# Moving the start addresses of the tiles that TensorE reads

## The chip, the cores and the metric

One core of one Trainium2 chip runs the whole program in one launch. The metric is the device time of one execution in microseconds (us). The kernel before has a median of 933.54 us over 2 runs (933.08 to 934.0).

## What is computed

Three layers follow each other: a gated linear attention (4 batches, 8 heads, 768 steps, head width 48), and two two-layer networks over 3072 tokens. Cut to what matters:

```python
for t in range(S):                       # attention
    state = f[:, :, t, :, None] * state + k_t (outer) v_t
    y[:, :, t] = q_t @ state
x = y as [3072 tokens, 384]
g = softplus(x @ w_in1);   x = g @ w_out1        # 384 -> 2048 -> 384
h = x @ w_in2                                     # 384 -> 2048
g = where(h >= 1, h, where(h <= -1, 0, (h + 1)**2 / 4))
out = g @ w_out2                                  # 2048 -> 384
```

## The kernel before

**Tiling.** Tokens go in six blocks of 512 per network. The 2048 hidden columns are 16 chunks of 128. For one chunk of one block, `hmm` (line 726) forms the hidden tile of 128 x 512 from the input (three pieces of 128 rows), `act1` or `act2` applies the nonlinearity on ScalarE and VectorE, and `second` (lines 800 to 802) multiplies the result into three output tiles that accumulate over the 16 chunks.

**Split numbers.** Every operand is kept as a high part and a low remainder, each in the type float32r: the input in `xh` and `xl` (one tile `xhl`), the hidden tile in `gh` and `gl` (three buffers each), the weights of chunk c in `w_h[c]` and `w_l[c]`. A product is three matmuls: low weights by high data, high weights by high data, high weights by low data. So a chunk of a block costs 9 matmuls in `hmm` and 9 in `second`, each with 128 x 128 weights and 512 moving columns. A weight tile holds 768 columns: 384 for the first product and 384 for the second. Block 0 of the first network is the exception: its operands are plain float32 (`xr2`, `g_0`, lines 726 and 805), with one matmul instruction pair in the place of three matmuls.

**Which weights are read where.** The first network uses `w_h[c]`, `w_l[c]` for all 16 chunks. The second network uses six further pairs, `wxh` and `wxl`, for chunks 0 to 5, and `w_h[c - 6]`, `w_l[c - 6]` for chunks 6 to 15. The `wx` tiles are allocated in `release()` in the space that the attention tiles leave.

**Order.** `Order` collects all operations with planned costs, due times and dependences between named tiles, schedules them once, and emits them in that order. The planned costs and the names do not depend on addresses. DMAs are all issued on SP's queue.

**Addresses.** Tiles of a pool lie one behind the other in each partition. Up to the small tiles at the end of the pool `const`, every tile is a multiple of 512 bytes long. In the placed program `xhl` starts at byte 2208, which is 160 modulo 512; so `w_h`, `w_l`, `stg`, `gh`, `gl`, `te`, `tu`, `tl`, `xr2`, `wa` and `g_0` all start at 160 modulo 512 as well. The attention tiles and later `acc`, `wxh` and `wxl` start at 352 modulo 512 (one attention tile, `ks1`, at 96).

The functions that the change touches:

Of the kernel before, what the change touches and what calls it, by code (L numbers as in the profile page):

```python
# [8 lines left out]
F32 = mybir.dt.float32  # L9
F32R = mybir.dt.float32r  # L10
# [7 lines left out]
P = 128  # L18
# [6 lines left out]
TB = 512  # L25

LAG, GB, TE = 2, 3, 2
# [289 lines left out]
def attn_moe_moe2_kernel(ctx: ExitStack, tc: tile.TileContext, q, k, v, f_logit,  # L317
# [8 lines left out]
    NFC = FF // P  # L326
# [4 lines left out]
    WN = NK * P + DM  # L331
# [5 lines left out]
    const = mstack.enter_context(tc.tile_pool(name="const", bufs=1))  # L337
# [7 lines left out]
    def buf(name, shape, n, dt=F32, pool=const):  # L345
        return [pool.tile(shape, dt, name=f"{name}{i}", tag=f"{name}{i}") for i in range(n)]
# [20 lines left out]
    H2 = [3, 5, 1]  # L367
    O2 = [4, 7, 6]

    xhl = const.tile([P, 2, NK, XR], F32R, name="xhl")  # L370
    xh, xl = xhl[:, 0], xhl[:, 1]
    yT = dram.tile([DM, NT], F32, name="yT")
    w_h = buf("wh", [P, WN], NFC, F32R)
    w_l = buf("wl", [P, WN], NFC, F32R)
    stg = buf("stg", [P, WN, 2] if wide else [P, WN], 2, I32 if wide else F32)
    g_h = buf("gh", [P, TB], GB, F32R)
    g_l = buf("gl", [P, TB], GB, F32R)
    t_e = buf("te", [P, TB], TE)
    t_u = buf("tu", [P, TB], 1)
    t_l = buf("tl", [P, TB], TE)  # L380
# [73 lines left out]
    w2x, acc = [], []  # L454
# [460 lines left out]
    def release():  # L915
        astack.close()
        wx = mstack.enter_context(tc.tile_pool(name="w2x", bufs=1))
        acc.append(wx.tile([P, TB], F32, name="acc"))
        nc.gpsimd.memset(acc[0], 0.0)
        for c in range(NX):  # L920
            w2x.append((wx.tile([P, WN], F32R, name=f"wxh{c}"), wx.tile([P, WN], F32R, name=f"wxl{c}")))

    conv2 = 0
    wnext = 2
# [1 line left out]
    for i in range(len(steps) + LAG):  # L926
        if i < len(steps):
            L, bi, t0, N, c = steps[i]
# [37 lines left out]
        if not released and ndone[0] == NU:  # L966
            released = True
            held = sorted((x for x in attn_keys if x[0] not in ("bank", "xh", "xl", "xr2", "x0", "te", "tl", "tu", "gh")), key=str)
            do("none", 0, release, held, [("w2x",), ("acc",)] + held)
            s_of[2, 0], s_of[2, 1] = load_w(2, 0), load_w(2, 1)  # L970
        j = i - LAG
        if j >= 0:
            L, bi, t0, N, c = steps[j]
# [66 lines left out]
```

## Time and profile before

| | |
|---|---|
| median of 2 runs | 933.54 us (933.08 to 934.0) |
| the profiled execution's own time | 934.49 us |
| its span, first to last instruction | 932.8 us |
| TensorE matmul (PE) busy | 915.6 us, 98% of the span |
| TensorE weight loads (PEld) busy | 711.9 us, 76% |
| VectorE (DVE) busy | 656.5 us, 70% |
| ScalarE (ACT) busy | 638.0 us, 68% |
| GpSimd (POOL) busy | 71.9 us, 8% |
| granted TensorE clock | 0.998 of full speed |

PE and PEld are one engine: a weight load runs beside the matmul before it. A matmul is pipelined: its record starts when it is taken up and ends when its last result is out, so the records of neighbours overlap, and a mean duration is longer than the time from one start to the next. The ends of matmuls in the records are modelled. What a stream of matmuls costs is read from the starts.

### The profile page before, as it was taken

What the parts mean: (1) busy time and instruction counts of PE and PEld (TensorE: products, weight loads), DVE (VectorE), ACT (ScalarE), POOL (GpSimd) and SP (SyncE); (2) the same over time, 40 slices, a digit from 0 to 9 for tenths busy, and PEclk for the clock granted to TensorE, in tenths of its full rate; (3) what the DMA queues carried; (4) which work ended last, traced back from release to release, by engine and by line L of the source; (5) the groups of instructions that cost most, each with busy time, mean ns of one, the idle gap of its engine ahead of it and who ended that gap; (6) DMA issues with size and microseconds to landing.
All of it is one profiled execution on the core that took longest, in us unless ns stands there. A gap on an engine that the chain in (4) does not pass through costs nothing.

```text
span 932.8 us, 14237 instructions
## 1 busy us (share of the span) xinstructions
PE 915.6 (98%) x5480; PEld 711.9 (76%) x5480; DVE 656.5 (70%) x1030; ACT 638.0 (68%) x1145; POOL 71.9 (8%) x91
## 2 busy tenths in 40 slices
PE   8999999999999999999999999999999999999997
PEld 7634458778778787788877888888888888888885
DVE  7999999877877777658999974464454554544542
ACT  5567689678777786667787778888864544544443
POOL 0001011001001000100020010020010010100000
PEclk9999999999999999999999999999999999999999
DMA  9577761412221221201343366665610200200001
GB/s 280 187 250 248 233 213 57 134 49 91 62 64 58 85 63 35 69 1 34 103 136 102 102 204 200 207 209 196 222 50 1 68 0 1 69 1 1 34 1 38
DMA packets 86540, 96.95 MB, mean 104 GB/s; under 512 B 4544, under 2 KB 66496, under 8 KB 86464
## 3 DMA queue, kind: packets, MB, share of 16 engines
q1 hardware_dynamic: 86464, 95.96, 31.7%
q8 instruction: 45, 0.74, 0.3%
q14 instruction: 31, 0.25, 0.1%
HBM read 80.22 MB, written 9.44 MB: 96 GB/s over the span
## 4 chain that ended last, share of the span: by engine, by line
PE 88%; DVE 6%; DMA 2%; issue 1%; ACT 1%; POOL 0%; SPq 0%; DVEq 0%; ACTq 0%
PE bank L726 40%; PE bank L800 12%; PE bank L801 12%; PE bank L802 12%; PE bank L805 3%; PE bank L625 3%; PE bank L667 1%; PE bank L681 1%; PE bank L654 1%; PE bank L672 1%; DVE gl L771 1%; DVE tl L763 1%; DMA xr<-yT 1%; DVE te L761 1%; PE bank L605 1%
## 5 line engine op out<-in xcount | busy, mean ns | idle before, releaser
L726 PE MATMUL bank<-xhl,wh 128*128 128x512 f32 x840 | 259.5, 390 | 0.0
L726 PEld LDWEIGHTS bank<-xhl,wh 128*128 128x128 f32 x840 | 157.7, 188 | 32.2 <-issue 0.2
L726 PE MATMUL bank<-xhl,wl 128*128 128x512 f32 x420 | 168.4, 401 | 0.4 <-DVE tl L763 0.4
L802 PE MATMUL bank<-gl,wh 128*128 128x512 f32 x420 | 163.7, 390 | 1.7 <-DVE gl L771 1.7
L800 PE MATMUL bank<-gh,wl 128*128 128x512 f32 x420 | 164.2, 391 | 0.0
L801 PE MATMUL bank<-gh,wh 128*128 128x512 f32 x420 | 163.5, 389 | 0.0
L424 ACT CAST gh<-tl 128x512 fp32r<-128x512 f32 x176 | 108.8, 618 | 73.2 <-DVE tl L786 51.1
L786 DVE TENSOR_TENSOR tl<-bank,te 128x512 f32<-128x512 f32 x96 | 66.3, 692 | 70.4 <-ACT te L785 70.4
L788 DVE TENSOR_TENSOR gl<-tl,gh 128x512 fp32r<-128x512 f32 x96 | 69.7, 727 | 61.8 <-ACT gh L424 60.2
L756 ACT ACTIVATE te<-bank 128x512 f32<-128x512 f32 x96 | 57.0, 594 | 60.9 <-PE bank L726 60.6
L726 PEld LDWEIGHTS bank<-xhl,wl 128*128 128x128 f32 x420 | 78.8, 188 | 22.0 <-DVE tl L763 2.9
L781 ACT ACTIVATE te<-bank 128x512 f32<-128x512 f32 x96 | 57.1, 594 | 54.0 <-PE bank L726 53.5
L802 PEld LDWEIGHTS bank<-gl,wh 128*128 128x128 f32 x420 | 78.8, 188 | 19.2 <-DVE gl L771 2.6
L800 PEld LDWEIGHTS bank<-gh,wl 128*128 128x128 f32 x420 | 78.8, 188 | 17.2 <-ACT gh L424 0.3
L801 PEld LDWEIGHTS bank<-gh,wh 128*128 128x128 f32 x420 | 78.9, 188 | 16.2
L785 ACT ACTIVATE te<-te 128x512 f32<-128x512 f32 x96 | 60.5, 631 | 41.5 <-DVE te L783 41.5
L761 DVE SCALAR_TENSOR_TENSOR te<-tu,te 128x512 f32<-128x512 f32 x96 | 68.1, 709 | 27.8 <-ACT tu L420 27.5
L783 DVE TENSOR_SCALAR te<-te 128x512 f32<-128x512 f32 x96 | 44.1, 460 | 55.3 <-ACT te L781 55.1
L771 DVE TENSOR_TENSOR gl<-tl,gh 128x512 fp32r<-128x512 f32 x80 | 56.6, 708 | 22.3 <-ACT gh L424 21.6
L763 DVE SCALAR_TENSOR_TENSOR tl<-bank,tl 128x512 f32<-128x512 f32 x96 | 65.7, 684 | 5.6 <-ACT tl L759 5.6
L726 PE MATMUL bank<-xhl,wxh 128*128 128x512 f32 x216 | 66.9, 391 | 0.0
L420 ACT ACTIVATE tu<-te 128x512 f32<-128x512 f32 x96 | 60.6, 631 | 2.3 <-DVE te L761 0.4
(115 smaller groups left out, 1378.6 us busy)
## 6 DMA issues: line engine op xcount, KB each, us to landing
stg<-in_moe_w_in_dram SPq DMA_DIRECT2D x64, 384.0 KB, 3.7
stg<-in_moe_w_out_dram SPq DMA_DIRECT2D x64, 384.0 KB, 4.4
t_f<-in_f_logit_dram SPq DMA_DIRECT2D x23, 256.0 KB, 3.5
t_k<-in_k_dram SPq DMA_DIRECT2D x23, 256.0 KB, 3.5
t_q<-in_q_dram SPq DMA_DIRECT2D x23, 256.0 KB, 3.7
vz<-in_v_dram SPq DMA_DIRECT2D x23, 256.0 KB, 3.9
wl<-wa SPq DMA_DIRECT2D x14, 384.0 KB, 3.0
yT<-xr SPq DMA_DIRECT2D x18, 256.0 KB, 3.3
```

Of the source, the lines that this page charges most:

```text
L420: "act": (c_act(n), lambda: nc.scalar.activation(out=o, in_=x, func=AF.Identity, bias=1.0))}
L424: "act": (c_act(n, ps), lambda: nc.scalar.copy(o(), x()))}
L726: nc.tensor.matmul(o, l, r, start=(j == 0), stop=(j == n - 1))
L761: do("dve", c_dve(N), lambda: nc.vector.scalar_tensor_tensor(out=e, in0=u, scalar=-1.0, in1=e, op0=ALU.add, op1=ALU.subtract), [ku, ke], [ke])
L763: do("dve", c_dve(N), lambda: nc.vector.scalar_tensor_tensor(out=l, in0=h, scalar=0.0, in1=l, op0=ALU.max, op1=ALU.add), [kb, kl], [kl])
L771: do("dve", c_dve(N), lambda: nc.vector.tensor_tensor(out=gl, in0=l, in1=gh.bitcast(F32), op=ALU.subtract), [kl, kgh], [kgl])
L785: do("act", c_act(N), lambda: nc.scalar.activation(out=r, in_=r, func=AF.Square), [kr], [kr])
L786: do("dve", c_dve(N), lambda: nc.vector.tensor_tensor(out=l, in0=h, in1=r, op=ALU.max), [kb, kr], [kl])
L788: do("dve", c_dve(N), lambda: nc.vector.tensor_tensor(out=gl, in0=l, in1=gh.bitcast(F32), op=ALU.subtract), [kl, kgh], [kgl])
L800: nc.tensor.matmul(o, ol, gh, start=(c == 0), stop=False)
L801: nc.tensor.matmul(o, oh, gh, start=False, stop=False)
L802: nc.tensor.matmul(o, oh, gl, start=False, stop=(c == NFC - 1))
```

## The change

The tiles get other start addresses; no instruction is added, removed or reordered by the source. An unused tile of 352 bytes is placed ahead of `xhl`, so that `xhl` starts at 0 modulo 512. Each weight tile becomes 32 bytes longer, each `gh` and `gl` tile 64 bytes longer, and the kernel uses slices of the old length. The `wx` tiles get the same 32 bytes.

```diff
+    const.tile([P, 88], F32, name="pad")
     xhl = const.tile([P, 2, NK, XR], F32R, name="xhl")
...
-    w_h = buf("wh", [P, WN], NFC, F32R)
-    w_l = buf("wl", [P, WN], NFC, F32R)
+    w_h = [x[:, 0:WN] for x in buf("wh", [P, WN + 8], NFC, F32R)]
+    w_l = [x[:, 0:WN] for x in buf("wl", [P, WN + 8], NFC, F32R)]
...
-    g_h = buf("gh", [P, TB], GB, F32R)
-    g_l = buf("gl", [P, TB], GB, F32R)
+    g_h = [x[:, 0:TB] for x in buf("gh", [P, TB + 16], GB, F32R)]
+    g_l = [x[:, 0:TB] for x in buf("gl", [P, TB + 16], GB, F32R)]
...
-            w2x.append((wx.tile([P, WN], F32R, name=f"wxh{c}"), wx.tile([P, WN], F32R, name=f"wxl{c}")))
+            w2x.append([wx.tile([P, WN + 8], F32R, name=f"wx{x}{c}")[:, 0:WN] for x in "hl"])
```

Adding up the lengths gives the starts after it, modulo 512: `xhl` 0; `w_h[c]` and `w_l[c]` 32c each; `stg` 0; `gh` 0, 64, 128; `gl` 192, 256, 320; `te`, `tu`, `tl`, `xr2`, `wa` and `g_0` 384; `wxh` of chunk c 64 + 64c and `wxl` 96 + 64c; the attention tiles 64 (`ks1` 320). In all 1,760 bytes more of each partition are used.

## Rows read from the trace of the kernel before

**Rows 1.** The page: busy us (share of the span) and instructions of two engines.
```profile
PE 915.6 (98%) x5480; PEld 711.9 (76%) x5480; DVE 656.5 (70%) x1030; ACT 638.0 (68%) x1145; POOL 71.9 (8%) x91
```

**Rows 2.** The page: chain that ended last, shares of the span by engine.
```profile
PE 88%; DVE 6%; DMA 2%; issue 1%; ACT 1%; POOL 0%; SPq 0%; DVEq 0%; ACTq 0%
```

**Rows 3.** Busy time by stretch: us, engines with instructions, granted clock, DMA share, GB/s.
```profile
0.00:112.00 112.00, 104.52 (x784) 60.44 (x784) 105.70 (x169) 69.30 (x116) 10.18 (x23) 1.00 0.75 239
112.00:485.00 373.00, 372.05 (x2774) 291.27 (x2773) 303.11 (x473) 289.18 (x517) 34.90 (x51) 1.00 0.26 82
485.00:545.00 60.00, 57.88 (x250) 46.16 (x250) 59.76 (x89) 44.37 (x77) 3.44 (x3) 1.00 0.35 113
545.00:932.80 387.80, 381.18 (x1677) 314.00 (x1675) 187.97 (x302) 235.21 (x437) 23.37 (x15) 1.00 0.25 85
```

**Rows 4.** Matmul groups by shape: count, busy us, mean ns of one, idle before.
```profile
L726 PE MATMUL bank<-xhl,wh 128*128 128x512 f32 x840 | 259.5, 390 | 0.0
L801 PE MATMUL bank<-gh,wh 128*128 128x512 f32 x420 | 163.5, 389 | 0.0
...
L726 PE MATMUL bank<-xhl,wxh 128*128 128x512 f32 x216 | 66.9, 391 | 0.0
L801 PE MATMUL bank<-gh,wxh 128*128 128x512 f32 x108 | 42.5, 394 | 0.0
...
L726 PE MATMUL bank<-xhl,wxl 128*128 128x512 f32 x108 | 42.3, 392 | 0.0
L802 PE MATMUL bank<-gl,wxh 128*128 128x512 f32 x108 | 41.9, 388 | 0.0
```

**Rows 5.** Timeline of PE, second network: start us, us; last matmul of a chunk.
```profile
569.31 0.39 PE L802 MATMUL bank<-gl,wh 128*128 128x512 f32 x1
...
593.79 0.39 PE L802 MATMUL bank<-gl,wh 128*128 128x512 f32 x1
...
606.11 0.39 PE L802 MATMUL bank<-gl,wxh 128*128 128x512 f32 x1
...
618.47 0.39 PE L802 MATMUL bank<-gl,wxh 128*128 128x512 f32 x1
```

**Rows 6.** Timeline of PE in the plain float32 block, six instructions merged.
```profile
103.69 2.74 PE L726 MATMUL bank<-xr,wl 128*128 128x512 f32 x6
```

**Rows 7.** The costliest groups of the page: the float32 matmuls of that block.
```profile
L726 PE MATMUL bank<-xr,wl 128*128 128x512 f32 x96 | 44.1, 595 | 0.6 <-ACT xr L424 0.6
```

**Rows 8.** Timelines of PE and PEld where the next weight load comes late.
```profile
162.34 0.39 PE L802 MATMUL bank<-gl,wh 128*128 128x512 f32 x1
162.65 0.30 PE L667 MATMUL bank<-am,vz 128*32 128x128 f32 x1
...
162.11 0.19 PEld L802 LDWEIGHTS bank<-gl,wh 128*128 128x128 f32 x1
162.65 0.38 PEld L667 LDWEIGHTS bank<-am,vz 128*32 128x32 f32 x16 [0.35 <-issue]
```

**Rows 9.** Timeline of PE after a stall, and its group in that window.
```profile
449.49 0.40 PE L726 MATMUL bank<-xhl,wh 128*128 128x512 f32 x1
449.73 0.39 PE L726 MATMUL bank<-xhl,wh 128*128 128x512 f32 x1
...
L726 PE MATMUL bank<-xhl,wh 128*128 128x512 f32 x1 | 0.4, 397 | 0.0
```

**Rows 10.** VectorE's split of a weight tile: count, busy us, mean ns, idle before.
```profile
L500 DVE TENSOR_TENSOR wl<-wa,wh 128x768 fp32r<-128x768 f32 x10 | 9.5, 953 | 0.1
L500 DVE TENSOR_TENSOR wxl<-wa,wxh 128x768 fp32r<-128x768 f32 x6 | 5.7, 949 | 0.6 <-ACT wxh L424 0.6
```

**Rows 11.** DMA issues: count, KB each, median us from issue to landing.
```profile
stg<-in_moe_w_in_dram SPq DMA_DIRECT2D x64, 384.0 KB, 3.7
wl<-wa SPq DMA_DIRECT2D x14, 384.0 KB, 3.0
```

## The prediction, made before the changed kernel was run

> **What bounds the kernel now.** I read the busy shares first: PE is busy for 98% of the span, the next engine, VectorE, for 70% [rows 1]. The chain that ended last says the same: 88% of it is PE [rows 2]. Then the stretches, since an average can hide a stage: PE is full in all four, and VectorE equals it only in two short ones, the first 112 us (105.70 of 112) and the 60 us between the networks (59.76 of 60) [rows 3]. So the time is the number of matmuls times the time from one matmul to the next, and an edit of addresses matters if it changes that interval. The granted clock is 1.00 in every stretch, the upper of the two levels (2.4 GHz) [rows 3], so the clock is no unknown.
>
> The matmuls that the change is about are the float32r ones. Eleven blocks (five of the first network, six of the second) of 16 chunks with 18 each are 3,168. Of these 648 read `wx` weights (6 blocks x 6 chunks x 18: one group of 216 and four of 108) and 2,520 read `w` weights (one group of 840 and four of 420) [rows 4].
>
> The interval comes from starts. Between the last matmuls of two `w` chunks, 569.31 and 593.79, lie six chunks or 108 matmuls: 24.48 / 108 = 226.7 ns. Between 606.11 and 618.47 lie three `wx` chunks or 54 matmuls: 12.36 / 54 = 228.9 ns [rows 5]. 3,168 matmuls at 227 ns are 719 us, 77% of the span.
>
> **A natural experiment in the trace.** In all of the kernel before, moving data and `w` weights start at the same address modulo 512, while `wx` weights start 192 bytes away from the moving data. That is the thing the change varies, and the price is there: 2.2 ns more per matmul, not less. The mean durations agree: 388 to 394 ns with `wx`, against 389 in the undisturbed `w` group [rows 4]. So a different start is not shown to be better; the only other start in the trace is slightly worse.
>
> Why the effect is small can be estimated from the shapes. One matmul reads 2,048 bytes per partition, so it passes every address modulo 512 four times; a weight load reads 512 bytes and passes each once. Whatever the two starts, the streams cross; the starts set only when.
>
> **The change part by part.**
>
> *Weights of the `w` chunks at 32c.* Chunk 0 of the first network and chunk 6 of the second (which reads tile 0) keep the offset of 0 to `xhl`: 5 x 18 + 6 x 18 = 198 matmuls, which I leave as they are (their `gh` and `gl` move too; the size of that is inside the bounds). The other 2,322 get an offset that is not 0. No row shows most of these offsets. From below: the `gl,wxh` group at 388 ns is the shortest, 1 ns under 389 [rows 4], so 2,520 x -1 = -2.5 us. From above: a matmul just after a stall, when load and matmul meet at another moment, took 397 ns and 0.24 us to the next start [rows 9]: 8 ns more, 2,520 x 8 = +20.2 us. The longest steady group, `gh,wxh` at 394 [rows 4], gives 2,520 x 5 = +12.6 us. I take 2.2 ns, the only steady value at an unequal offset: 2,322 x 2.2 = **+5.1 us**.
>
> *Weights of the `wx` chunks.* They go from one unequal offset to others. Bounds: all at the `w` interval, 648 x -2.2 = -1.4 us; all at 397 ns against their mean of 391, 648 x 6 = +3.9 us. I take **0**.
>
> *Moving data at 0 in place of 160.* No float32r matmul in the trace has moving data elsewhere, so its own price is unknown. Above nothing I have no row but the 397 already counted; below, the float32 block sets the bound: six instructions last 2.74 us [rows 6], less one duration of 0.595 [rows 7] that is 2.145 / 5 = 429 ns per instruction with two passes of 512 columns, 214.5 ns per pass. A float32r pass takes 12.2 ns more. But that block's moving tiles and weights stand at 160 too, and pay nothing for it. And a matmul that starts at 162.34 with no weight load beside it until 162.65 has the same 0.39 us as every other [rows 8]. So neither 160 as such nor the load beside it explains the 12 ns as far as rows go (with the reserve that ends are modelled). I take **0**, and keep the 12 ns for a rival.
>
> The Trainium skill, "TensorE: Matmul & The Clock Gate", section "Step-by-step: what each phase is for", says that TensorE reads moving data and weights through two independent ports, so that loading the next weights takes nothing from the running matmul. By that the sum would be 0. It speaks against the change. The trace agrees where a matmul without a load is no shorter [rows 8], and disagrees by the 2.2 ns of `wx` [rows 5].
>
> *The float32 block and the attention.* 192 instructions with moving data at 384 and weights at 32c. They have slack: two passes per load, and 214.5 ns per pass. At 5 ns per instruction it would be 1 us; I take 0. The attention tiles all move together by 224 bytes, so their offsets to each other stay.
>
> *VectorE, ScalarE, DMA.* VectorE's split takes 953 ns into tiles at 160 and 949 at 352 [rows 10]: nothing. PE hides them except between the networks, where VectorE fills 60 us [rows 3]; 1% there is 0.6 us. Weight transfers land in 3.7 and 3.0 us [rows 11], and DMA holds 2% of the chain [rows 2]: a tenth more or less on that, 932.8 x 0.02 x 0.1, is 2 us at most. The same DMAs go out on SP's queue in the same order, and no wait is added, since the planner's costs and tile names don't depend on addresses; the unused tile emits no instruction.
>
> **Sum.** +5.1 us. The profiled execution took 934.49 us, 1.7 more than its span and 0.95 more than the median of 933.54. Against the median: 933.54 + 5.1 = 938.6. The likeliest case's own range, from the lower bounds together (-2.5 - 1.4) to the steady upper bound (+12.6 and 1.7 for `wx`), is 929.6 to 947.8.
>
> **The rivals.**
>
> *No effect.* Within a nanosecond the interval doesn't depend on starts, and `wx` is slower for another reason, such as its place high in the partition. For: the crossing argument. Against: nothing else separates `wx` from `w` in the trace. Time: 933.5.
>
> *Faster.* The 12.2 ns between float32r and the float32 pass is a collision of equal or ill-placed starts, and goes: 2,520 x 12.2 + 648 x 14.4 = 40 us. Between the networks VectorE takes over [rows 3], where 250 matmuls would have brought 3 us. 933.5 - 37 = 897 at best, 915 if half of the offsets profit. For: the gap exists, and float32r is the only kind that shows it. Against: [rows 8], and `wx` with an unequal offset is no faster. The skill's page named above, section "Back-to-back issue gap", gives N / 2.4 + 2.5 ns, 215.8 for 512 columns; by it the interval of 226.7 leaves 11 ns to win, which the float32 pass agrees with and no float32r row here shows.
>
> *Slower.* Many of the 15 new offsets hold load and matmul in the bad meeting that now occurs only after stalls, at 397 ns [rows 9]. The place is every float32r matmul; the price 20.2 + 3.9 = 24 us, 957.6. It decides from a mean of 18.7 / 3,168 = 5.9 ns per matmul upward. For: the `wx` groups already range over 388, 392 and 394. Against: even they average under 3 ns.
>
> *It doesn't do what it says.* Other starts than added up would need a placement that rounds by more than 32 bytes; then the time is the no-effect one, and its chance is in that.
>
> **How the numbers follow.** About 2% (18.7 us) is what a measurement of this kernel can tell from no change. Forecast 0.50, no effect 0.22, faster rival 0.16 (of which 0.02 stays within 2%), slower rival 0.12. So faster 0.14, same 0.74, slower 0.12. The range of 928 to 953 takes in the likeliest case, no effect and the near part of the slower rival; it leaves out the faster rival and the far end of the slower one, 0.2 together.
>
> **What would show it.** The durations by tile: `wh` and `wl` groups near 391 instead of 389, `wx` near 391, and PE's interval in six `w` chunks near 24.7 us instead of 24.48. Chunks should differ from each other, since each has its own offset. The float32 instruction stays at 429 ns from start to start. I am wrong if the float32r interval falls below 225 ns (the 12 ns were a matter of address), or if the mean passes 233 (the bad meeting is the common one). If PE's interval is unchanged and the time is not, the cause lies in DMA or in the stretch between the networks.

## The result, and the profile after

The changed kernel takes 945.76 us (945.57 to 945.94, 2 runs) against 933.54 us: a ratio of 1.0131, 95% interval 1.0087 to 1.0174. It is slower by 12.2 us, a small loss but one clear of the noise. Its profiled execution has a span of 943.8 us, 11.0 us more than before. In its code, line 726 has become 728, and 800 to 802 have become 802 to 804.

The page of the changed kernel: busy us, share and instructions of the engines, and the chain's shares by engine (answers to [rows 1, 2]).

```profile
PE 928.4 (98%) x5480; PEld 713.1 (76%) x5480; DVE 656.9 (70%) x1030; ACT 639.4 (68%) x1145; POOL 76.2 (8%) x91
...
PE 93%; DVE 3%; DMA 1%; issue 1%; ACT 1%; POOL 0%; SPq 0%; DVEq 0%; POOLq 0%
```

The same number of instructions, 12.8 us more of PE, and VectorE, ScalarE and the weight loads within 1.4 us of what they were. PE's share of the chain grows from 88% to 93%. The time is in the matmuls.

The busy time by stretch of the changed kernel (columns as in [rows 3]) says the same: PE stays full and the granted clock stays 1.00. The stretches are cut by time, so they don't hold the same work as before.

```profile
0.00:112.00 112.00, 104.95 (x784) 60.96 (x785) 105.89 (x170) 69.30 (x116) 12.43 (x23) 1.00 0.74 241
112.00:485.00 373.00, 372.20 (x2754) 287.90 (x2753) 299.93 (x468) 286.10 (x511) 33.08 (x50) 1.00 0.26 81
485.00:545.00 60.00, 58.78 (x253) 46.98 (x252) 59.74 (x89) 45.05 (x78) 7.53 (x3) 1.00 0.31 99
545.00:943.80 398.80, 392.46 (x1693) 317.22 (x1691) 191.36 (x307) 238.92 (x442) 23.20 (x15) 1.00 0.25 85
```

The groups of float32r matmuls (answer to [rows 4]): count, busy us, mean ns of one, idle before.

```profile
L728 PE MATMUL bank<-xhl,wh 128*128 128x512 f32 x840 | 263.2, 394 | 0.0
L728 PE MATMUL bank<-xhl,wl 128*128 128x512 f32 x420 | 169.9, 405 | 0.0
L802 PE MATMUL bank<-gh,wl 128*128 128x512 f32 x420 | 165.8, 395 | 0.0
L804 PE MATMUL bank<-gl,wh 128*128 128x512 f32 x420 | 165.7, 394 | 1.2 <-DVE gl L773 1.2
L803 PE MATMUL bank<-gh,wh 128*128 128x512 f32 x420 | 165.6, 394 | 0.0
L728 PE MATMUL bank<-xhl,wxh 128*128 128x512 f32 x216 | 67.6, 394 | 0.0
...
L804 PE MATMUL bank<-gl,wxh 128*128 128x512 f32 x108 | 42.6, 394 | 0.0
L728 PE MATMUL bank<-xhl,wxl 128*128 128x512 f32 x108 | 42.5, 394 | 0.0
L803 PE MATMUL bank<-gh,wxh 128*128 128x512 f32 x108 | 42.5, 394 | 0.0
```

Before, the `w` groups stood at 389 to 391 ns and the `wx` groups between 388 and 394. Now all stand near 394. The one exception, `xhl,wl`, holds some 40 matmuls of about 500 ns that open a chunk, in both kernels, and has risen likewise, from 401 to 405. Before it was:

```profile
L726 PE MATMUL bank<-xhl,wl 128*128 128x512 f32 x420 | 168.4, 401 | 0.4 <-DVE tl L763 0.4
```

Some 4 ns on 2,520 matmuls and some 2.3 ns on 648 make 11.6 us, against 11.0 us more span. The starts in the two traces say the same: the 3,123 intervals from one float32r matmul to another right behind it add up to 719.7 us before and 731.2 after.

The timeline of PE gives the interval. These are the same four matmuls of the second network as in [rows 5].

```profile
573.53 0.39 PE L804 MATMUL bank<-gl,wh 128*128 128x512 f32 x1
...
598.63 0.39 PE L804 MATMUL bank<-gl,wh 128*128 128x512 f32 x1
...
611.16 0.40 PE L804 MATMUL bank<-gl,wxh 128*128 128x512 f32 x1
...
623.66 0.40 PE L804 MATMUL bank<-gl,wxh 128*128 128x512 f32 x1
```

Six `w` chunks: 25.10 us / 108 = 232.4 ns from start to start, where it was 226.7. Three `wx` chunks: 12.50 / 54 = 231.5 ns, where it was 228.9. So in both the interval has grown as the durations have: a steady 389 ns stands for 226.7 ns, and a duration longer by d for an interval longer by d. The experiments below are read by that.

"Offset" below means the start of the weights less the start of the moving data, so `wx` had 192 before. The direction counts: 192 and 64 are not the same offset.

The float32 block didn't move (answer to [rows 6], timeline of PE):

```profile
103.51 2.74 PE L728 MATMUL bank<-xr,wl 128*128 128x512 f32 x6
```

### The profile page after: what moved, and what is told of

Its sections match the earlier page's. It is cut to its first block, busy times and chain, and to the rows that moved or that the text cites. A ratio compares the mean times of both kernels' runs of the same rounds, so it can differ in the third digit from the quotient of the medians.

```text
span 943.8 us, 14237 instructions
## 1 busy us (share of the span) xinstructions
PE 928.4 (98%) x5480; PEld 713.1 (76%) x5480; DVE 656.9 (70%) x1030; ACT 639.4 (68%) x1145; POOL 76.2 (8%) x91
## 4 chain that ended last, share of the span: by engine, by line
PE 93%; DVE 3%; DMA 1%; issue 1%; ACT 1%; POOL 0%; SPq 0%; DVEq 0%; POOLq 0%
PE bank L728 42%; PE bank L802 13%; PE bank L804 13%; PE bank L803 13%; PE bank L807 3%; PE bank L627 3%; PE bank L669 1%; PE bank L683 1%; PE bank L656 1%; PE bank L674 1%; PE bank L607 1%; DMA stg<-in_moe_w_in_dram 1%; PE bank L678 0%; PE bank L530 0%; DMA t_f<-in_f_logit_dram 0%
## 5 line engine op out<-in xcount | busy, mean ns | idle before, releaser
L728 PE MATMUL bank<-xhl,wh 128*128 128x512 f32 x840 | 263.2, 394 | 0.0
L804 PE MATMUL bank<-gl,wh 128*128 128x512 f32 x420 | 165.7, 394 | 1.2 <-DVE gl L773 1.2
L803 PE MATMUL bank<-gh,wh 128*128 128x512 f32 x420 | 165.6, 394 | 0.0
```

Of the source, the lines that this page charges most:

```text
L728: nc.tensor.matmul(o, l, r, start=(j == 0), stop=(j == n - 1))
L803: nc.tensor.matmul(o, oh, gh, start=False, stop=False)
L804: nc.tensor.matmul(o, oh, gl, start=False, stop=(c == NFC - 1))
```

## The experiments

The question is which part of the change costs, and what about an address counts: where the moving data starts (theory B in the expectations), where it starts against the weights (A), that tiles differ from chunk to chunk (A3), or where a tile lies in the partition (C). Eleven kernels were run, each the kernel before with one part of the change or one other edit. Where a kernel has other line numbers, its lines are those of `hmm` and of the three matmuls in `second`.

### The pad alone

```diff
+    const.tile([P, 88], F32, name="pad")
     xhl = const.tile([P, 2, NK, XR], F32R, name="xhl")
```

> Only the unused tile of 352 bytes is added: moving data, w weights and hidden tiles all start at 0 modulo 512, and wx weights keep their 192 bytes of offset. If only the offset between moving data and weights counts (theory A), nothing changes: 933.5 us, w groups at 389 ns and wx groups at 391 ns as before. If the place of the moving data counts (theory B: 0 is a worse start than 160), the w groups go to the 391.7 ns that the changed kernel shows for chunk 6 of its second network, where both stand at 0: 2.7 ns x 2,520 = +6.8, about 940 us.

Measured: 933.7 us, ratio 1.000 (0.999 to 1.001). Its groups:

```profile
L802 PE MATMUL bank<-gh,wh 128*128 128x512 f32 x420 | 163.5, 389 | 0.0
...
L727 PE MATMUL bank<-xhl,wxl 128*128 128x512 f32 x108 | 42.3, 392 | 0.0
```

They are those of before to the nanosecond, the `wx` groups with their offset of 192 included. Moving data and `w` weights all at 0 are as good as all at 160: theory B falls.

### The weights alone

```diff
-    w_h = buf("wh", [P, WN], NFC, F32R)
+    w_h = [x[:, 0:WN] for x in buf("wh", [P, WN + 8], NFC, F32R)]
...
(w_l and the wx tiles likewise; no pad, gh and gl as before)
```

> Only the weight tiles are 32 bytes longer (w and wx); the moving data and the hidden tiles stay at 160 modulo 512. Theory A: every chunk but the first has another offset to the moving data, and most of the cost of the change comes back: w groups at 393 to 395 ns, 943 to 946 us. Theory B: the moving data hasn't moved, so the w groups stay at 389 to 390 ns and the time at 933 to 936 us.

Measured: 947.87 us, ratio 1.0156 (1.0139 to 1.0173). Its groups:

```profile
L726 PE MATMUL bank<-xhl,wh 128*128 128x512 f32 x840 | 263.2, 394 | 0.0
...
L801 PE MATMUL bank<-gh,wh 128*128 128x512 f32 x420 | 165.8, 395 | 0.0
```

With all moving data left where it was, the whole price is there: theory A, and a little over the 943 to 946 us it gave.

The trace of this run also holds every offset in steps of 32 bytes, since the weights of chunk c start 32c bytes further on than the moving data, modulo 512. These are the mean intervals of the first network's chunks, taken from the starts, with intervals of 262 ns and more, and the ones right behind them, left out as waits: 230.4 and 230.0 ns at offsets of 0 and 256, 230.3 and 229.8 at 192 and 448, and 232.5 to 233.7 at the other twelve. Two things can be read from them. A chunk and the one 256 bytes further on agree within 0.5 ns, for all eight pairs. And no chunk keeps the 226.7 ns: even the chunks whose own starts are equal pay some 3 ns among neighbours whose starts are not.

### The hidden tiles alone

```diff
-    g_h = buf("gh", [P, TB], GB, F32R)
+    g_h = [x[:, 0:TB] for x in buf("gh", [P, TB + 16], GB, F32R)]
...
(g_l likewise)
```

> Only the gh and gl tiles are 64 bytes longer (they start at 160, 224, 288, 352, 416, 480 modulo 512); weights and xhl stay at 160, wx at 224. Theory A: the matmuls of the first product stay at 389 ns with w weights, those of the second go to 392 to 395 ns, as their moving data is no longer where the weights are: 1,584 x 4 ns = +6, about 939.5 us. Theory B: starts other than 160 cost, so the second product pays too, but by its own buffer and not by the chunk; the two theories differ in the first product with wx weights, now 64 instead of 192 bytes off: A leaves room for a change there, B has none.

Measured: 941.87 us, ratio 1.0092 (1.0075 to 1.0109). Its groups:

```profile
L726 PE MATMUL bank<-xhl,wh 128*128 128x512 f32 x840 | 260.4, 391 | 0.0
...
L802 PE MATMUL bank<-gl,wh 128*128 128x512 f32 x420 | 165.8, 395 | 1.4 <-DVE gl L771 1.4
...
L801 PE MATMUL bank<-gh,wh 128*128 128x512 f32 x420 | 165.2, 393 | 0.0
L726 PE MATMUL bank<-xhl,wxh 128*128 128x512 f32 x216 | 67.9, 395 | 0.0
```

That is 2.4 us more than the 939.5 that theory A gave. The second product pays 3 to 5 ns with `w` weights. `xhl` with `wx` pays too: its own starts changed only in their offset, from 192 to 64, and the group goes from 391 to 395 (its neighbours in the second product changed as well). The first product with `w` weights, whose own starts are still equal, rises by 1 ns: it follows a group of the second product and needs some matmuls to come back. By the starts, the first four of its nine matmuls take 230.4 ns and the last five 228.1, where both parts had between 227 and 228 before. The parts don't add up: 1.56% and 0.92% apart, 1.31% together.

### The wx tiles brought to the others

```diff
+        wx.tile([P, 80], F32, name="padx")
         acc.append(wx.tile([P, TB], F32, name="acc"))
```

> The kernel before with one unused tile of 320 bytes ahead of acc, so that the wx tiles start at 160 modulo 512 like all other operands. Theory A: the wx groups fall from 391.3 to 389 ns and their intervals from 228.9 to 226.7 ns: 648 x 2.2 = -1.4 us, about 932.1 us. Theory C (the wx tiles are slower because of where they lie in the partition, not because of the offset): they stay at 391, 933.5 us.

Measured: 932.5 us, ratio 0.9987 (0.9978 to 0.9997). Its groups:

```profile
L726 PE MATMUL bank<-xhl,wxh 128*128 128x512 f32 x216 | 66.5, 389 | 0.0
...
L802 PE MATMUL bank<-gl,wxh 128*128 128x512 f32 x108 | 42.0, 389 | 0.0
```

Theory C falls: the same tiles, 320 bytes further on, are as fast as the `w` tiles. A gain of 1.2 us (0.1%) that neither kernel has.

### Constant offsets of 256 and 128 bytes

```diff
+    const.tile([P, 64], F32, name="pada")      # ahead of w_h: 256 bytes
+    const.tile([P, 64], F32, name="padb")      # behind w_l
+        wx.tile([P, 112], F32, name="padx")    # ahead of acc: wx 128 bytes off xhl
```

> The kernel before with every w tile 256 bytes off the moving data modulo 512 and every wx tile 128 bytes off, the same for all chunks; xhl, gh and gl stay at 160. If any unequal start breaks the steady rhythm of matmul and weight load, but a constant one settles (theory A1), each chunk settles on one repeating pattern, the w groups between 391 and 396 ns and the wx groups likewise: +5 to +17 us, 938 to 950. If starts count modulo 256 or 128 only (theory A2), the w groups stay at 389 and the time at 933.5 (modulo 256) or 932.1 with wx at 389 too (modulo 128). If the change costs because its starts differ from chunk to chunk (theory A3), a constant offset costs no more than wx did before, 391: 938 at most.

Measured: 937.07 us, ratio 1.0039 (1.0026 to 1.0051). Its groups:

```profile
L803 PE MATMUL bank<-gh,wh 128*128 128x512 f32 x420 | 163.6, 389 | 0.0
L728 PE MATMUL bank<-xhl,wxh 128*128 128x512 f32 x216 | 67.7, 395 | 0.0
```

An offset of 256 costs nothing. An offset of 128 costs 6 ns against equal starts, although it is the same for all chunks. So 256 counts as equal, and 128 doesn't. The span is 3.5 us longer than before. 648 `wx` matmuls at 4 ns over before are 2.6 us of it; the `w` matmuls of the second network that stand next to a `wx` chunk pay most of the rest (by the starts 227.1 to 229.3 ns in chunks 6 to 8, 14 and 15, against 226.7 to 226.9 in the others).

### An offset of 16 bytes

```diff
-    g_h = buf("gh", [P, TB], GB, F32R)
+    g_h = [x[:, 4:4 + TB] for x in buf("gh", [P, TB + 128], GB, F32R)]
...
(g_l and xhl likewise; wx tiles equal to w as above)
```

> The kernel before with all moving data (xhl, gh, gl) 16 bytes behind the weights modulo 512, wx included (they stand with the w tiles here). If the offset counts in bytes, a small one is like any other: groups at 391 to 396 ns, 938 to 950 us. If it counts in steps of 32 bytes or more (the finest that the change tried), 16 bytes are as good as 0: all groups at 389 and the time 932.1 us, as with the wx tiles made equal.

Measured: 945.4 us, ratio 1.013 (1.0113 to 1.0147), as slow as the change. Its groups:

```profile
L801 PE MATMUL bank<-gh,wh 128*128 128x512 f32 x420 | 165.6, 394 | 0.0
L726 PE MATMUL bank<-xhl,wxh 128*128 128x512 f32 x216 | 67.6, 394 | 0.0
```

One small offset, the same everywhere (the weights 16 bytes before the data, 240 modulo 256 in the counting above), costs what 16 different ones cost. Theory A3 falls with it.

### The change in steps of 256 bytes

```diff
-    w_h = buf("wh", [P, WN], NFC, F32R)
+    w_h = [x[:, 0:WN] for x in buf("wh", [P, WN + 64], NFC, F32R)]
...
(gh, gl and wx tiles likewise, and the tile ahead of acc of the wx experiment)
```

> The change done in steps of 256 bytes: every w_h, gh, gl and wx tile is 256 bytes longer, so that neighbours differ by 256 modulo 512, and an unused tile brings wx to 160 or 416; xhl stays at 160. If starts count modulo 256 (as the w groups at 389 with an offset of 256 suggest), nothing of the change's cost comes back and the gain of equal wx tiles stays: all groups at 389 in the steady state, 932 us, ratio about 0.9985. If the change costs because tiles start at different places at all, or because they change from chunk to chunk (theory A3), it costs like the change: 941 to 946.

Measured: 932.37 us, ratio 0.998 (0.997 to 0.999). Its groups:

```profile
L801 PE MATMUL bank<-gh,wh 128*128 128x512 f32 x420 | 163.5, 389 | 0.0
...
L726 PE MATMUL bank<-xhl,wxh 128*128 128x512 f32 x216 | 66.5, 389 | 0.0
```

Tiles that differ from chunk to chunk, and moving data that differs from buffer to buffer, cost nothing as long as the differences are multiples of 256. It equals the kernel with equal `wx` tiles and beats both kernels of the case, by 0.2% against the one before.

### Moving data read from one address

Each float32r matmul reads one column 512 times.

```diff
-            XH, XL = xh[:, :, xo:xo + N], xl[:, :, xo:xo + N]
+            XH, XL = (x[:, :, xo:xo + 1].broadcast_to([P, NK, N]) for x in (xh, xl))
...
(gh and gl likewise)
```

> The kernel before, but every float32r matmul reads its 512 moving columns from one column (step 0), so its output is not the reference's; counts, shapes, weights and waits are the same. If the 12 ns that a float32r pass takes over a float32 pass come from the moving stream walking through addresses and meeting the weight load (theory W), the interval falls to about 214.5 ns and the w groups from 389 to 377 ns: 38 us less, 895 to 900. If they belong to the float32r pass itself (theory I), the groups stay at 388 or 389 and the time near 933; what can go then is only the extra of wx, 1.5 us.

Measured: 906.58 us, ratio 0.9711 (0.9692 to 0.9731). Two groups, then two rows of its timeline of PE:

```profile
L802 PE MATMUL bank<-gh,wh 128*128 128x512 f32 x420 | 160.4, 382 | 0.0
...
L726 PE MATMUL bank<-xhl,wxh 128*128 128x512 f32 x216 | 64.5, 380 | 0.0
...
650.00 0.38 PE L801 MATMUL bank<-gh,wl 128*128 128x512 f32 x1
...
651.30 0.38 PE L726 MATMUL bank<-xhl,wxl 128*128 128x512 f32 x1
```

Between the two rows lie six matmuls: 1.30 / 6 = 216.7 ns, 10 ns less than before, and `wx` is no slower than `w` any more. Theory W gave 214.5 and 895 to 900 us, so it is 2 ns and some 7 us too low, but the larger part of the 12 ns goes with the walk of the moving data.

The 216.7 ns are a mean of two values. Over the whole trace the three matmuls of a product take 215.0, 220.0 and 215.0 ns to the next start, in their order: low weights by high data, high by high, high weights by low data. Two of three are thus within 0.5 ns of the float32 pass. The middle one is followed by a load of the same weights again and by a change of the moving tile; why it takes 5 ns more isn't shown.

### Weights read from one address

```diff
+            one = lambda x, m: x[:, m * P:m * P + 1].broadcast_to([P, P])
...
(every float32r weight load reads one column 128 times)
```

> The kernel before, but every float32r weight load reads its 128 columns from one column (step 0), so its output is not the reference's. Theory W (the weight load's walk through addresses meets the moving read): the wx extra of 2.2 ns vanishes or changes, since the load stays at one address: w and wx groups alike, 932 us; if the load also causes the 12 ns, the groups fall to 377 and the time to 895 to 900. Theory I: w groups stay at 389.

Measured: 944.43 us, ratio 1.0117 (1.0096 to 1.0137). Neither theory gave that. Its groups:

```profile
L803 PE MATMUL bank<-gl,wh 128*128 128x512 f32 x420 | 166.6, 397 | 1.6 <-DVE gl L772 1.6
...
L802 PE MATMUL bank<-gh,wh 128*128 128x512 f32 x420 | 164.2, 391 | 0.0
```

A load that stays in one place is worse than one that walks from an equal start. So a price is paid without any walk of the load; what part the walk has in the other kernels, this run doesn't say. The price is again not the same along a product: by line it is 396, 391 and 397 ns.

### Moving data walking through 256 bytes only

```diff
+            see = lambda x: x[:, None, 0:64].broadcast_to([P, 8, 64])    # the first 64 columns, eight times
```

> The kernel before, but every float32r matmul reads the first 64 of its 512 moving columns eight times (256 bytes per partition instead of 2,048), so its output is not the reference's. If the 10 ns that a fixed address saved belong to walking through one period of 256 bytes (theory S), the interval stays at 226.7 ns and the time at 933. If they belong to going on to new addresses beyond a period (theory R), it falls to about 216.7 as with one address: 906.6.

Measured: 933.72 us, ratio 0.9997 (0.9985 to 1.0008). Its groups:

```profile
L805 PE MATMUL bank<-gh,wh 128*128 128x512 f32 x420 | 163.5, 389 | 0.0
...
L805 PE MATMUL bank<-gh,wxh 128*128 128x512 f32 x108 | 42.5, 394 | 0.0
```

Eight times through the same 256 bytes is the same as once through 2,048, down to the `wx` group's 394: theory S.

### Moving data in pieces of 16 bytes, 256 apart

```diff
+            see = lambda x: x.rearrange("p (a b t) -> p b a t", a=8, t=4)
```

> The kernel before, but every float32r matmul reads its 512 moving columns in another order: four columns (16 bytes), then the four that lie 256 bytes further on, eight times, then the next sixteen bytes; its output columns come in that order, so it is not the reference's. Under theory S with starts counting modulo 256, the moving stream now stays eight pieces long at one place modulo 256 before it goes on, so it meets the weight load differently: the interval leaves 226.7, down to 216.7 at best (906) or up to 235 (958). Under theory R every piece is a new place and the interval rises above 226.7 or stays.

Measured: 1087.47 us, ratio 1.164 (1.1614 to 1.1665), far outside what either theory gave.

```profile
L726 PE MATMUL bank<-xhl,wh 128*128 128x512 f32 x840 | 303.0, 444 | 0.0
...
L805 PE MATMUL bank<-gh,wh 128*128 128x512 f32 x420 | 186.4, 444 | 0.0
```

55 ns more per matmul. It fits S in that places 256 apart are not as good as neighbours when read one after the other, but the shape of the access (short pieces) changed with it, and the two aren't told apart.

## Why the prediction was right, and where it was off

*What bounds the kernel:* right. The loss is PE's, at the same clock of 1.00. Against the signs that the prediction named: six `w` chunks take 25.10 us, where it gave near 24.7, and the chunks do differ from each other, between 230.3 and 233.3 ns in the second network (by the starts). The mean of 232.4 ns in those six chunks stays just under the 233 that would have made it wrong.

*The natural experiment:* right in sign. That the 192 bytes of offset, and not the place, made `wx` slower is now shown by the kernel with the `wx` tiles moved: the rival of no effect rested on the place, and falls.

*Weights at 32c:* this is the term that was mis-sized. I took 2.2 ns for every unequal offset because 192 was the only one in the trace. It is the cheapest of those measured: 394 to 395 ns at offsets of 64, 128 and 240, where 192 has 391. On the mean of the groups the price was 4 ns, 10 us in the place of 5.1. The bounds that stood beside it (5 ns at 394, 8 ns at 397) held it, in part by luck. The groups at 388 and 394 [rows 4] are not the far ends of what an offset can cost: by the starts in that trace, the three matmuls of a product with `wx` take 229, 232 and 226 ns in turn, one repeating pattern at one offset, and 394 is its longest third. That other offsets have 394 as their mean, nothing in that trace said.

The 198 matmuls that were left as they are paid too: in the changed kernel, chunk 6 of the second network takes 230.3 ns, with its hidden tiles moved and unequal neighbours around it.

*The wx tiles:* I took 0. They lost 2.3 ns, 1.5 us, since they left the cheapest offset. Inside the bound of 3.9 us.

*Moving data at 0:* 0, as the pad alone shows (ratio 1.000).

*Why the effect is small:* half right. The estimate from the shapes went by 512 bytes; the chip repeats after 256. That the streams cross in any case is in line with the loads from one address, which are no better, but not shown by them. But the start does more than set when they cross: from equal starts the matmuls fall into a steady 226.7 ns, from others into longer patterns, such as the 229, 232, 226 of `wx`.

*The 12 ns to the float32 pass:* the faster rival had a true gap and a wrong remedy. With the moving data held at one address 10 of the 12.2 ns go; no start address tried, and no walk through memory, brought the mean of a stream under 226.7.

*What can be told from no change:* the prediction took 2%, 18.7 us, as the least that a measurement of this kernel can tell. The runs can tell much smaller differences: moving the `wx` tiles gained 0.13%, with an interval of the ratio of 0.9978 to 0.9997.

*The slower rival:* its 397 ns turn up among the matmuls (836 of 3,168 last 397 to 400 ns, where it was 95) but not as the mean; the mean of some 4 ns stays under the 5.9 that it needed.

*The skill's rule:* the Trainium skill, "TensorE: Matmul & The Clock Gate", section "Step-by-step: what each phase is for", has moving data and weights read through independent ports, so that a load takes nothing from the running matmul. The weights alone, moved by multiples of 32 bytes, cost 1.56%: for these float32r matmuls the measurement decides against the sum of 0 that the prediction drew from the rule. Whether it is the load of the next weights that takes something from the running matmul isn't shown.

**What stays open.** Why 256 bytes, and which reads get in each other's way, isn't shown. The matmul without a load beside it [rows 8] was as long as the others, and a load at one address made things worse, so "the next load slows the running matmul" is not settled as the mechanism. Offsets under 16 bytes weren't tried, and those of 32, 96, 160 and 224 only in streams that mix offsets. That a matmul pays for its neighbours' offsets, and for how long, was seen but not tested by itself.

## What to carry to other kernels

Where a stream of float32r matmuls of 512 columns bounds a kernel, let every moving tile and every weight tile start at the same address modulo 256 bytes; in this kernel an unequal start cost 1 to 3% of each interval, and putting the last unequal tiles right gained 0.1 to 0.2%. No other kernel was tried, and no other shape of float32r matmul. Look in the trace for two groups of the same shape whose mean durations differ by a few nanoseconds: here `wx` at 391 beside `w` at 389 told the sign of the change before it was run, and one unused tile took the difference away. A single unequal value in a trace is a sign, not a size: price the others by the far bound as well.

## What the runs showed of the hardware

- Starts of moving data and weights count modulo 256 bytes for these matmuls: offsets of 0 and 256 give 389 ns, 64 and 128 give 395, 240 (weights 16 bytes before the data) gives 394, 192 gives 391. In the kernel with the weights alone moved, the eight pairs of chunks 256 bytes apart agree within 0.5 ns.
- In a stream that mixes offsets, matmuls with equal starts pay as well: 230 ns in place of 226.7 in that kernel.
- A float32r matmul whose moving data stays at one address takes 216.7 ns from start to start in the mean (215.0, 220.0 and 215.0 along a product) in place of 226.7. The Trainium skill, "TensorE: Matmul & The Clock Gate", section "Back-to-back issue gap", gives N / 2.4 + 2.5 ns as the gap of an isolated matmul, which is 215.8 ns for 512 columns. Of the float32r streams here only the one whose moving data doesn't walk comes within a nanosecond of that in its mean.
- A walk through 256 bytes costs as much as one through 2,048: 933.72 us against 934.26 for the kernel before in the same session.
- The plain float32 matmuls of this kernel don't mind: six instructions take 2.74 us in the kernel before, with moving data and weights at the same start, and in the changed one, where they mostly stand apart; the mean of all 96 goes from 595 to 596 ns.
